# Four attention layers on one core: another order of the first block's maxima, and another opening of layer 0

## The chip, the cores and the metric

The kernel runs on one core of a Trainium2 chip. The metric is the device time of one execution in microseconds (us); the time of a version is the median of its runs. One execution was also profiled, and the profile's times count from the start of its span.

## What is computed

The input x holds 2048 tokens of 576 numbers (float32). Four layers follow each other, A, B, A, B, and each adds attention on the normalised x:

```python
x = x + A(layernorm(x)); x = x + B(layernorm(x))   # and once more
# A: q, k, v of 32 heads of 18 numbers each from wqkv
# B: 32 query heads, but one k and one v for all of them
p = softmax(einsum("bhqd,bhkd->bhqk", q, k) * 18 ** -0.5)
y = einsum("bhqk,bhkd->bhqd", p, v) @ wo
```

All 2048 x 2048 scores of every head are computed; nothing is masked.

## The kernel before

**Precision.** Operands are split into a high and a low part (fp32r), and a product takes the sum of high by high, high by low and low by high. A weight part is copied to its high part by one engine (`hi`) and its low part is subtracted by another (`lo`) in `load_w`, which `load_a` calls for layer A's weights, part by part and chunk by chunk of 128 rows (five chunks `c`; L229 is the subtraction).

**A layer's front.** x is normalised in 16 chunks of 128 tokens (`stats`, `scaled`: VectorE L309 to L321, with GpSimd L313 and L314 for the root), and each chunk is transposed by TensorE into PSUM (`transposed`: four products into a tile of the e banks, L272, and a fifth, L273, into `oacc` or, for chunks 1 and 3 of layer 0, into a tile of its own). `split_rows` brings it to SBUF as `xx` or `yx`: ScalarE copies the high part (L264, L265), VectorE subtracts for the low part (L266, L267). `advance` transposes the next chunk and prepares those behind it. `project(T, t)` forms 128 columns `t` of q and k for quarter `T` (512 tokens) by 14 products (`TERMS`, L439) in a PSUM tile psq; with `half` it does 256 tokens only. ScalarE then copies the result (ev, L447), VectorE or GpSimd makes its low part (L456, or L454 from the copy evr, L453), and SyncE stores it to DRAM (L499 to L503). In layer 0 `key_diff` adds a copy k0 (L473) on ScalarE for the key tiles. k and q come back from DRAM as rows of `big`, by columns, through `load_k` and `load_q` (L545).

**Maxima and exponentials.** For the softmax, each block `u` of 512 queries needs the maximum of its scores over all 2048 keys, per query. A product psm (`max_mm`, L613; `qc` counts 128 queries, `kb` 512 keys) gives 128 x 512 scores, and VectorE reduces them (L620). When 32 of them are there for a block, `max_final` takes the negated maximum (L752), GpSimd splits it (hl), `max_store` transposes it (L761) and stores it to DRAM (m_d, L763), and `max_rows` loads it as two further rows of `big` (L767), so that the product pse (L776) yields scores less the maximum. ScalarE takes the exponential (L785), and the product with the values gathers in `oacc` (L806). The main loop runs over 16 pairs of heads and four blocks, and its order is written out by hand in `UNIT`.

**Before the main loop.** The first `LEAD` = 14 groups of four psm have no exponentials beside them. `woven(max_pairs, left, every)` weaves them into the projections that are left: `beat` counts products of 512 columns, and after each `every` of them one group is issued. In A layers all 14 lie in the stretch `fill`; in B layers five lie in quarter 2, six in quarter 3 (`woven`, called with 5 and 10, then 1, 2 and 2 with 7, 6 and 6), and the rest in `fill`. Their order in B layers is the list `m_first` of (u, qc, kb): two entries for both heads of the pair make one group of four, called #1 to #14 here.

**PSUM.** Eight banks: three for `mtile`, four for `etile`, one for `oacc`. `etile` serves psq of the fill, the transposes and pse; `mtile` serves psm and the other psq. Each takes its banks in turn, and a new tile waits until the readers of the bank's last tile are done.

## Time and profile before

| | us |
|---|---|
| median of 3 runs | 5605.41 |
| the runs | 5609.56, 5603.79, 5605.41 |
| the profiled execution | 5606.94 |
| its span in the profile | 5605.2 |
| TensorE busy | 5579.4 |
| VectorE busy | 4943.0 |
| ScalarE busy | 4936.3 |
| GpSimd busy | 1741.9 |

The span leaves out 1.74 us around it. In a timeline row stand the start, the duration, the engine with line, operation, output and inputs, a count where rows are merged, and in brackets how long the engine stood idle before and what ended that. PE is TensorE, DVE VectorE, ACT ScalarE, POOL GpSimd, SPq SyncE's queue of DMA issues. A duration of merged rows runs to the modelled end of the last one, so that consecutive rows of PE overlap by a pipeline's depth.

### The profile page before, as it was taken

What the parts mean: (1) busy time and instruction counts of PE and PEld (TensorE: products, weight loads), DVE (VectorE), ACT (ScalarE), POOL (GpSimd) and SP (SyncE); (2) the same over time, 40 slices, a digit from 0 to 9 for tenths busy, and PEclk for the clock granted to TensorE, in tenths of its full rate; (3) what the DMA queues carried; (4) which work ended last, traced back from release to release, by engine and by line L of the source; (5) the groups of instructions that cost most, each with busy time, mean ns of one, the idle gap of its engine ahead of it and who ended that gap; (6) DMA issues with size and microseconds to landing.
All of it is one profiled execution on the core that took longest, in us unless ns stands there. A gap on an engine that the chain in (4) does not pass through costs nothing.

```text
span 5605.2 us, 138270 instructions
## 1 busy us (share of the span) xinstructions
PE 5579.4 (100%) x53372; PEld 2835.7 (51%) x53372; DVE 4943.0 (88%) x9513; ACT 4936.3 (88%) x9884; POOL 1741.9 (31%) x2236
## 2 busy tenths in 40 slices
PE   9999999999999999999999999999999999999999
PEld 7644444444844444444686444444448444444446
DVE  5799999998699999999747999999987999999995
ACT  3599999999389999999726999999992999999996
POOL 3142323234233232333421332323242333333332
PEclk9999999999999999999999999999999999999999
DMA  6311111111421000001253111111114201010102
GB/s 226 120 47 38 37 39 36 39 36 27 128 68 24 23 21 23 20 23 25 61 188 104 50 36 38 37 39 36 37 31 136 56 23 24 23 24 20 24 14 80
DMA packets 258556, 291.59 MB, mean 52 GB/s; under 512 B 132700, under 2 KB 172892, under 8 KB 248176
## 3 DMA queue, kind: packets, MB, share of 16 engines
q1 hardware_dynamic: 257896, 282.75, 18.0%
q8 instruction: 419, 6.86, 0.5%
q14 instruction: 241, 1.97, 0.1%
HBM read 158.77 MB, written 119.86 MB: 50 GB/s over the span
## 4 chain that ended last, share of the span: by engine, by line
PE 97%; ACT 1%; DVE 1%; DMA 0%; issue 0%; SPq 0%; POOL 0%; ACTq 0%; DVEq 0%; POOLq 0%
PE oacc L806 38%; PE pse L776 23%; PE psm L613 21%; PE psn L280 6%; PE psq L439 6%; PE psd L605 3%; ACT pt L785 1%; PE ps L272 0%; DVE mx L620 0%; DMA big<-m_d 0%; DMA m_d<-tr 0%; PE oacc L273 0%; SPq L763 0%; DVE mxd L620 0%; ACT side L785 0%
## 5 line engine op out<-in xcount | busy, mean ns | idle before, releaser
L620 DVE TENSOR_REDUCE mxd<-psm 128x1 f32<-128x512 f32 x5952 | 3750.1, 683 | 181.5 <-PE psd L605 64.9
L785 ACT ACTIVATE pt<-pse 128x512 f32<-128x512 f32 x6584 | 3578.4, 628 | 28.3 <-PE pse L776 1.5
L613 PE MATMUL psm<-big 62*128 62x512 f32 x7200 | 2504.4, 444 | 0.6
L776 PE MATMUL pse<-big 64*128 64x512 f32 x8192 | 2409.1, 431 | 7.2 <-DMA big<-m_d 3.1
L806 PE MATMUL oacc<-pt,vbuf 128*19 128x192 f32 (+6 forms) x20244 | 1794.5, 379 | 1.2 <-DVE oc L202 1.0
L776 PEld LDWEIGHTS pse<-big 64*128 64x128 f32 x8192 | 1209.2, 184 | 893.8 <-ACT pt L785 517.6
L613 PEld LDWEIGHTS psm<-big 62*128 62x128 f32 x7200 | 1132.7, 184 | 676.7 <-DVE mxd L620 262.2
L806 PE MATMUL oacc<-side,vbuf 128*19 128x64 f32 (+6 forms) x5004 | 1402.5, 377 | 0.0
L785 ACT ACTIVATE side<-pse 128x512 f32<-128x512 f32 x1608 | 998.4, 621 | 5.9
L202 POOL TENSOR_SCALAR hl<-neg 128x8 fp32r<-128x8 f32 x256 | 50.5, 197 | 2746.7 <-DVE neg L752 2746.7
L806 PEld LDWEIGHTS oacc<-pt,vbuf 128*19 128x19 f32 x20244 | 447.8, 97 | 604.8 <-issue 488.7
L617 DVE CUSTOM_DVE_ANT_0 side<-psm,side 128x512 f32<-128x512 f32 x992 | 681.1, 687 | 37.0 <-PE psm L613 8.6
L610 ACT ACTIVATE side<-psd 128x512 f32<-128x512 f32 x992 | 601.3, 648 | 1.3 <-PE psd L605 1.3
L806 PE MATMUL oacc<-pt,vy 128*19 128x384 f32 (+2 forms) x5700 | 587.2, 417 | 0.0
L829 POOL TENSOR_TENSOR rl<-lt,mone 128x8 f32<-128x8 f32 x256 | 422.9, 1652 | 350.2 <-DMA lt<-os 350.2
L806 PE MATMUL oacc<-side,vy 128*19 128x384 f32 (+2 forms) x1404 | 455.7, 415 | 0.0
L605 PE MATMUL psd<-kd,big 54*128 54x512 f32 x992 | 428.0, 472 | 0.0
L806 PEld LDWEIGHTS oacc<-side,vbuf 128*19 128x19 f32 x5004 | 317.4, 97 | 146.4 <-issue 119.8
L447 ACT ACTIVATE ev<-psq 128x512 fp32r<-128x512 f32 (+1 forms) x112 | 66.9, 598 | 319.1 <-PE psq L439 266.6
L842 POOL TENSOR_TENSOR os<-os,rb 96x512 f32<-96x512 f32 x256 | 328.2, 1282 | 19.8 <-DMA rb<-r_d 19.8
L820 POOL TENSOR_TENSOR os<-os,side 96x512 f32<-96x512 f32 x240 | 307.2, 1280 | 20.0
L202 POOL TENSOR_SCALAR os<-side 32x512 f32<-32x512 f32 x480 | 293.7, 612 | 40.1 <-POOL hl L756 0.4
(93 smaller groups left out, 3310.3 us busy)
## 6 DMA issues: line engine op xcount, KB each, us to landing
big<-qk_d SPq DMA_DIRECT2D x180, 432.0 KB
qk_d<-ev SPq DMA_DIRECT2D x96, 512.0 KB
qk_d<-ev SPq DMA_DIRECT2D x120, 256.0 KB
rb<-r_d SPq DMA_DIRECT2D x512, 36.0 KB
o_d<-os SPq DMA_DIRECT2D x512, 36.0 KB
m_d<-tr SPq DMA_DIRECT2D x1024, 2.0 KB
o<-o_d SPq DMA_DIRECT2D x64, 256.0 KB
big<-m_d SPq DMA_DIRECT2D x512, 4.0 KB
```

What stands on the lines that cost most here:

```text
L202: eng.tensor_scalar(dst, src, 1.0, 0.0, op0=OP.mult, op1=OP.add)
L280: nc.tensor.matmul(ps, lhs[:, xc, :], wsm[:, wc, h * 288:(h + 1) * 288], start=i == 0, stop=i == len(TERMS) - 1)
L439: nc.tensor.matmul(ps[:n].rearrange("p (u t) -> p u t", u=2)[:, us], w[:, wc, :n], xts[T][:, us, xc, :], start=(xc, wc) == TERMS[0], stop= ...
L605: nc.tensor.matmul(ps, q[b:b + 3 * DH, c0:c0 + P], kds[p if is_a else 0][b:b + 3 * DH], start=True, stop=True)
L610: nc.scalar.activation(r, ps, AF.Relu)
L613: nc.tensor.matmul(ps, q[b:b + KM, c0:c0 + P], k[b:b + KM, kb * 512:(kb + 1) * 512], start=True, stop=True)
L617: nc.vector.tensor_tensor_reduce(out=r, in0=ps, in1=r, scale=1.0, scalar=-3.0e38, op0=OP.add, op1=OP.max, accum_out=mx[:, r0:r0 + 1])
L620: nc.vector.reduce_max(mx[:, r0:r0 + 1], ps, axis=AX.X)
L776: nc.tensor.matmul(e, k[r:r + KE, kc * P:(kc + 1) * P], q[r:r + KE, u * 512:(u + 1) * 512], start=True, stop=True)
L785: nc.scalar.activation(pt, e, AF.Exp, scale=SCALE)
L806: nc.tensor.matmul(oacc[j:j + DH + 1, cs], v_of(kc)[:, 2 * p + a if is_a else 0, :], pts[p, u, i][:, cs], start=kc < 2 and c0 == 0, stop=k ...
L829: nc.gpsimd.tensor_tensor(rl, lts.pop((p, u)), mone, op=OP.pow)
```

## The change

1. `m_first` of the B layers lists block 0 whole before block 1's later keys, and `max_store` and `max_rows` of that block are called after 42 and 48 products rather than 46 and 50.
2. In each group of four psm before the main loop the first takes an `etile` (before: the fourth), the other three an `mtile`.
3. `FREE`, which sets how many beats the groups of `fill` are to be done ahead of its end, is 8 in A layers and stays 4 in B layers.
4. Layer 0 begins with half products of three tiles of columns, not two, with the transposes of chunks 2 and 3 between them; the whole product of tile 2 in quarter 0 goes.
5. GpSimd subtracts all five low parts of layer 0's first weight part; VectorE did two of them.
6. Layer 0's chunk 7 is transposed after tile 7 of quarter 0 rather than after tile 8.

```diff
-FREE = 4
+FREE = 8, 4
...
-        m_first = [] if is_a else ([(0, i // 2, i % 2) for i in range(8)] + [(1, i // 2, i % 2) for i in range(4)] +
-                                   [(0, i, 2) for i in range(4)] + [(1, i // 2, i % 2) for i in range(4, 6)] +
-                                   [(0, i, 3) for i in range(4)] + [(1, i // 2, i % 2) for i in range(6, 8)] +
-                                   [(1, i, 2) for i in range(4)] + [(1, i, 3) for i in range(4)])
+        def block(u, kb, qcs=range(4)):
+            return [(u, qc, kb) for qc in qcs]
+
+        m_first = [] if is_a else (block(0, 0) + block(0, 1) + block(1, 0) + block(0, 2) + block(0, 3) +
+                                   block(1, 1) + block(1, 2) + block(1, 3))
...
             for a in range(2):
-                max_mm(a, etile if m_done[0] % 4 == 3 else mtile)
-            if not is_a and m_done[0] == 46:
+                max_mm(a, mtile if m_done[0] % 4 else etile)
+            if not is_a and m_done[0] == 42:
                 max_store(0, 0)
-            elif not is_a and m_done[0] == 50:
+            elif not is_a and m_done[0] == 48:
                 max_rows(0, 0)
...
-                    load_a(c, (part,), nc.scalar, nc.gpsimd if part == 0 and c < 3 else nc.vector)
+                    load_a(c, (part,), nc.scalar, nc.vector if part else nc.gpsimd)
...
-            for terms in (TERMS_LO[:9], TERMS_LO[9:]):
-                for t in (0, 1):
-                    project(0, t, half=0, terms=terms)
-            more("trans", 4)
+            for t in range(3):
+                project(0, t, half=0, terms=TERMS_LO[:9])
+            for t in range(3):
+                project(0, t, half=0, terms=TERMS_LO[9:])
+                if t < 2:
+                    more("trans", 3 + t)
             ready(0)
             finish_loads(5)
-            for t in (0, 1):
+            for t in range(3):
                 project(0, t, half=1)
...
-                ts = range(0 if T or layer else 2, 9) if T < 3 else (6, 7, 8, 0, 4)
+                ts = (None, *range(3, 9)) if T + layer == 0 else range(9) if T < 3 else (6, 7, 8, 0, 4)
...
-                project(T, t, not is_a and T >= 2)
+                if t is not None:
+                    project(T, t, not is_a and T >= 2)
...
+                elif T + layer == 0:
+                    moves = i in (0, 2, 4, 5)
                 else:
-                    moves = i % 2 != (T + layer == 0) if is_a else i < 4
+                    moves = i % 2 if is_a else i < 4
...
-        woven(max_pairs, left, (work - FREE) / left)
+        woven(max_pairs, left, (work - FREE[layer % 2]) / left)
```

Three places show how the rows move. First TensorE in layer 0's opening, from the low terms to the second half products; psq is a projection's tile, ps_260 and ps_270 (before), ps_265 and ps_280 (changed) are the transposes of chunks 2 and 3. Before:

```order
L439 MATMUL psq<-yx,big 128x256 x13
L439 MATMUL psq<-yx,big 128x256 [waits Pool_49] x3
L439 MATMUL psq<-yx,big 128x256 [waits DVE_49] x2
L439 MATMUL psq<-yx,big 128x256 x5
L272 MATMUL ps_260<-ident,xh 128x128 [waits DVE_49]
...
L272 MATMUL ps_270<-ident,xh 128x128 [waits DVE_49]
...
L439 MATMUL psq<-yx,big 128x256 x19
L439 MATMUL psq<-yx,big 128x512 x14
```

With the change:

```order
L439 MATMUL psq<-yx,big 128x256 x22
L439 MATMUL psq<-yx,big 128x256 [waits Pool_49] x5
L272 MATMUL ps_265<-ident,xh 128x128 [waits DVE_49]
...
L439 MATMUL psq<-yx,big 128x256 x5
L272 MATMUL ps_280<-ident,xh 128x128 [waits DVE_49]
...
L439 MATMUL psq<-yx,big 128x256 x5
...
L439 MATMUL psq<-yx,big 128x256 x33
```

Nine more half products stand ahead of chunk 3's transposes, four of them ahead of chunk 2's, and the 14 products of 512 columns are gone.

Second, ScalarE at the end of quarter 0 in layer 0, where L264 and L265 split chunk 7 and the L447 and L473 beside them are the copies of tile 8. Before:

```order
L473 ACTIVATE k_614<-psq 128x512 [waits DMAHW6_49,DMAHW0_49,Pool_49]
L447 ACTIVATE ev<-psq 128x512 [waits DMAHW1_49,DMAHW7_49,PE_49,Pool_49]
L473 ACTIVATE k_637<-psq 128x512 [waits DMAHW6_49,Pool_49]
L264 ACTIVATE xx<-ps_642 128x4x128 [waits PE_49]
L265 ACTIVATE xx<-oacc 128x128 [waits PE_49]
```

With the change:

```order
L264 ACTIVATE xx<-ps_633 128x4x128 [waits PE_49]
L265 ACTIVATE xx<-oacc 128x128 [waits PE_49]
L447 ACTIVATE ev<-psq 128x512 [waits DMAHW1_49,DMAHW7_49,PE_49,Pool_49]
L473 ACTIVATE k_672<-psq 128x512 [waits DMAHW6_49,Pool_49]
L447 ACTIVATE ev<-psq 128x512 [waits DMAHW2_49,PE_49,Activation_49]
```

The split of chunk 7 moved past tile 8's two copies.

Third, TensorE in quarter 3 of layer 1, at groups #9 and #10; the DMA semaphores are those of the loads of k's columns 1536 to 2047, one for each head. Before:

```order
L613 MATMUL psm_23418<-big_81 128x512 [waits DVE_49]
L613 MATMUL psm_23421<-big_81 128x512 [waits DVE_49]
L613 MATMUL psm_23424<-big_81 128x512 [waits DVE_49]
L613 MATMUL psm_23427<-big_81 128x512 [waits PE_49,Activation_49]
L439 MATMUL psq_23411<-xx_23096,big_81 128x512 x6
L613 MATMUL psm_23436<-big_81 128x512 [waits DMAHW6_49,DVE_49]
L613 MATMUL psm_23439<-big_81 128x512 [waits DMAHW7_49,DVE_49]
L613 MATMUL psm_23442<-big_81 128x512 [waits DVE_49]
L613 MATMUL psm_23445<-big_81 128x512
```

With the change:

```order
L614 MATMUL psm_23432<-big_81 128x512 [waits DMAHW6_49,DVE_49]
L614 MATMUL psm_23435<-big_81 128x512 [waits DMAHW7_49,DVE_49]
L614 MATMUL psm_23438<-big_81 128x512 [waits DVE_49]
L614 MATMUL psm_23441<-big_81 128x512 [waits DVE_49]
L439 MATMUL psq_23425<-xx_23110,big_81 128x512 x6
L614 MATMUL psm_23450<-big_81 128x512 [waits PE_49,Activation_49]
L614 MATMUL psm_23453<-big_81 128x512 [waits DVE_49]
L614 MATMUL psm_23456<-big_81 128x512 [waits DVE_49]
L614 MATMUL psm_23459<-big_81 128x512 [waits DVE_49]
```

The first product that waits for these loads moved from group #10 to group #9, one group ahead.

## The prediction

> **What bounds the kernel now.** I read the page first (busy times, then the chain that ended last), then TensorE's waits, then the timeline around each wait that the change touches, then the stretches' granted clock.

> ```profile
> span 5605.2 us, 138270 instructions
> PE 5579.4 (100%) x53372; PEld 2835.7 (51%) x53372; DVE 4943.0 (88%) x9513; ACT 4936.3 (88%) x9884; POOL 1741.9 (31%) x2236
> PE 97%; ACT 1%; DVE 1%; DMA 0%; issue 0%; SPq 0%; POOL 0%; ACTq 0%; DVEq 0%; POOLq 0%
> ```

> TensorE is busy for 5579.4 of 5605.2 us: 25.8 us of idle time are all that any reordering can win, and the changed kernel's TensorE does the same work (14 products of 512 columns become 28 of 256). TensorE's waits by line:

> ```profile
> PE pse L776 <- DMA big<-m_d: 3.1, 4, 1.4
> PE psq L439 <- ACT xx L264: 1.9, 1, 1.9
> PE psq L439 <- DVE ev L456: 0.7, 1, 0.7
> ```

> The reader is to see how little there is: the change aims at the first (the maxima of a layer's first block must be back in DRAM before the first exponential's product) and at the second (chunk 7 in layer 0). I take its parts in program order.

> **Layer 0's opening.** TensorE:

> ```profile
> 12.03 5.38 PE L439 MATMUL psq<-yx,big 128*128 128x256 f32 x24 [0.22 <-DVE yx L267]
> 17.80 0.60 PE L272 MATMUL ps<-ident,xh 128*128 128x128 f32 x4
> 20.64 5.90 PE L439 MATMUL psq<-yx,big 128*128 128x256 f32 x34 [0.23 <-DVE yx L267]
> 26.37 0.60 PE L272 MATMUL ps<-ident,xh 128*128 128x128 f32 x4
> 26.81 0.27 PE L273 MATMUL oacc<-ident,xh 128*128 128x128 f32 x1
> 27.80 2.58 PE L439 MATMUL psq<-yx,big 128*128 128x512 f32 x10 [0.72 <-DVE ev L456]
> ```

> VectorE and GpSimd beside it:

> ```profile
> 7.31 3.00 POOL L229 TENSOR_TENSOR big<-raw,big 128x384 fp32r<-128x384 f32 x3
> 19.57 0.69 DVE L266 TENSOR_TENSOR yx<-ps,yx 128x512 fp32r<-128x512 f32 x1
> 20.61 0.82 DVE L309 BATCH_NORM_STATS2 st<-xo 128x6 f32<-128x288 f32 x2
> 27.06 1.89 DVE L456 TENSOR_TENSOR ev<-psq,ev 128x512 fp32r<-128x512 f32 x3
> ```

> GpSimd's two further low parts cost 1.00 us each and end at 7.31 + 5.00 = 12.3; their first reader comes after 27 half products, four of which ran before 12.03, so near 17.0: hidden by more than 4 us, and free. VectorE's two additions go, but VectorE waits for ScalarE's split of chunks 2 and 3 later on, so nothing comes of it.

> A product of 512 columns takes 0.2325 us (3.72 us for 16, in the next part's first two rows). From 20.64 to 26.37 stand 20 half and 14 full ones: (5.73 - 3.26) / 20 = 0.124 us a half one. Chunk 3's transposes now follow nine more half products, 9 x 0.124 = 1.1: they start at 18.9 instead of 17.80 and end at 19.5. ScalarE's copy (0.6) then ends at 20.1, and VectorE's split of chunk 3 starts at 20.13 instead of 19.57: **+0.56**. Behind it VectorE is busy without a gap to the low half of tile 0's result at 27.06, and in the same order after the change, so that ends at 28.3 and tile 3's first product, which needs its PSUM bank, starts at 28.35 instead of 27.80. TensorE meanwhile has less to do: 34 half products from 21.14 end at 25.4, the transposes at 26.1. So its idle time of 0.72 us becomes about **2.3**, and the work moved forward (14 x 0.124 = 1.7 us) is only waited out here. Bounds: nothing lost if ScalarE is quicker (0), or all of it and a slow clock (below).

> **Chunk 7.**

> ```profile
> 44.82 3.88 PE L439 MATMUL psq<-yx,big 128*128 128x512 f32 x16
> 48.54 0.60 PE L272 MATMUL ps<-ident,xh 128*128 128x128 f32 x4
> 46.64 0.29 DVE L267 TENSOR_TENSOR xx<-oacc,xx 64x128 fp32r<-64x128 f32 x1
> 48.79 0.60 ACT L447 ACTIVATE ev<-psq 128x512 fp32r<-128x512 f32 x1 [0.92 <-POOL wsm L229]
> 50.52 0.59 ACT L264 ACTIVATE xx<-ps 128x512 fp32r<-128x512 f32 x1
> 51.17 4.14 PE L439 MATMUL psq<-xx,big 128*128 128x512 f32 x10 [1.92 <-ACT xx L264]
> ```

> The wait of 1.92 us is ScalarE's order: chunk 7's split stands behind tile 8's two copies. The change puts it ahead of them, so this wait goes. What is late next: tile 8's 14 products (3.26 us) now come behind the transposes. Tile 7 ends at 48.54 - 3.26 + 0.55 = 45.8; four transposes to 46.3; the fifth writes oacc, which VectorE frees at 46.93 + 0.55 = 47.5 when it has read chunk 6 (a **new wait of 1.2 us**, with tile 8 queued behind it); tile 8 runs from 47.6 to 50.9, and the next quarter follows at once. 50.9 against 51.17: **-0.27** for the whole opening, -1.92 + 1.2 + 0.55, less 0.1 where pipelined ends overlap.

> **The clock.**

> ```profile
> 47.87:51.28 3.41, 1.49 (x10) 1.07 (x9) 1.63 (x5) 1.85 (x4) 3.18 (x5) 1.00 1.00 361
> 51.28:54.69 3.41, 3.41 (x9) 2.67 (x10) 3.33 (x7) 0.00 (x1) 2.97 (x7) 0.50 1.03 387
> 1563.38:1566.79 3.41, 3.41 (x14) 1.21 (x15) 1.13 (x4) 2.10 (x5) 0.40 (x2) 0.50 0.57 146
> 1566.79:1570.21 3.42, 3.42 (x28) 1.08 (x30) 2.28 (x4) 1.97 (x4) 0.00 (x0) 0.50 0.60 144
> ```

> The columns are the stretch, then PE, PEld, DVE, ACT and POOL, then PEclk. The clock is halved over 3.41 us behind a stretch with 1.49 us of TensorE work, and over 6.83 us in layer 1's start. The stretches begin 1512.10 us apart, 443 times 3.4134, so they lie on a grid that no edit here controls: 1.7 us lost per halved stretch of TensorE work, about 5 in this run. I leave those in the sum (the new idle times may put others in the place of the removed one) and keep 1.7 per new gap for the range. [...]

> **Layers 0 and 2: FREE and the tiles of the group.**

> ```profile
> 217.61 0.59 ACT L453 ACTIVATE evr<-psq 128x512 f32<-128x512 f32 x1
> 218.09 2.08 ACT L785 ACTIVATE pt<-pse 128x512 f32<-128x512 f32 x4
> 218.26 0.50 PE L776 MATMUL pse<-big 64*128 64x512 f32 x2 [0.59 <-ACT evr L453]
> ```

> The third pse waits 0.59 us for a PSUM bank that the last tile's copy frees; with the etile first in the group it comes one product later. But ScalarE goes from that copy straight into the exponentials (217.61 + 0.59, then 218.09) and TensorE's next work needs them, so ScalarE's chain sets the pace and the wait moves down it. Maxima moved up to four beats (4 x 0.2325 = 0.93 us) meet a VectorE with idle time. Between -0.59 and +0.25 each; I take -0.05 each, near none: **-0.1**.

> **Layers 1 and 3: the order of the maxima.** Groups of four products (psm, two blocks for two heads) are woven into the projections, #9 at 1543.60 and #10 at 1545.86.

> ```profile
> 1540.99 1.21 SPq L545 DMA_DIRECT2D big<-qk_d  x2
> 1543.60 0.73 PE L613 MATMUL psm<-big 62*128 62x512 f32 x4
> 1545.86 0.73 PE L613 MATMUL psm<-big 62*128 62x512 f32 x4
> 1543.60:1545.86 2.26, 2.26 (x12) 1.35 (x12) 1.75 (x4) 0.00 (x0) 0.72 (x1) 1.00 0.89 321
> 1553.05 6.63 DVE L620 TENSOR_REDUCE mx<-psm 128x1 f32<-128x512 f32 x11
> 1556.71 2.16 DMA big<-m_d
> 1558.91 0.73 PE L776 MATMUL pse<-big 64*128 64x512 f32 x4 [0.65 <-DMA big<-m_d]
> ```

> Block 0's maxima now end with group #10 instead of #11, and the stores follow 4 maxima sooner; at 0.6 us each (6.63 us for 11, without a gap) that covers 0.65, so the wait at 1558.91 goes. But the price is new: k's last quarter (columns 1536 to 2047) was first read by #10, and now **#9 reads it**. Its loads are issued at 1540.99 to 1542.20. #10 met no wait, so they land before 1545.86. The nearest landing, of 4 KB rows, took 2.16 us from its issue: not before 1542.20 + 2.16 = 1544.36. A wait at #9 of 0.76 to 2.26, then. The queues were busy to 0.89 in exactly this stretch, and these loads move 108 KB each: I take the upper part, **1.9**. Behind #9 in TensorE's order stand all later projections and groups, and VectorE, which is fed by them, slides as well. Net in layer 1: 1.9 - 0.65 = **+1.25**.

> ```profile
> 4334.42 1.22 SPq L545 DMA_DIRECT2D big<-qk_d  x2
> 4337.02 0.73 PE L613 MATMUL psm<-big 62*128 62x512 f32 x4
> 4339.28 0.73 PE L613 MATMUL psm<-big 62*128 62x512 f32 x4
> 4352.15 0.90 PE L776 MATMUL pse<-big 64*128 64x512 f32 x4 [0.47 <-DMA big<-m_d]
> ```

> Layer 3 repeats it: issue ends at 4335.64, so the wait at 4337.02 is 0.78 to 2.26; 1.9 - 0.47 = **+1.43**.

> **Sum.** The profiled execution took 5606.94 us (span 5605.2 and 1.74 around it): 5606.94 - 0.27 - 0.1 + 1.25 + 1.43 = 5609.25. It stands 1.53 above the median of the runs shown, so against that median **5607.7**.

> **Rivals.**
> - *It does what it is meant to.* The loads land by 0.76 after #9's turn or sooner, the waits for m_d and xx go. For it: 2.16 us sufficed for small rows. Against it: a busy queue. Two waits of 0.4 instead of 1.9 and one halved stretch less: 5607.7 - 3.0 - 1.7 = 5603.
> - *The clock takes more.* The gaps of 2.3 at 26 us and 1.9 at each #9 each may put one stretch at half speed: two of three give 5607.7 + 3.4 = 5611.1. For it: 51.28. Against it: the stretch must begin so that most of a gap lies in one.
> - *Clearly slower.* In layers 1 and 3 the ramp behind #9 is paced by VectorE; if #9's gap halves the clock and TensorE, in short pieces between waits, doesn't win it back until the first pse, 15 us later (1558.91), each layer loses four stretches of 1.7: 5607.7 + 13.6 = 5621. It decides from five halved stretches in all (8.5 us); the trace has two in a row at most.
> - *The edits do nothing at all*, since all of them sit behind other work: 5605.4. Against it: #9's operand is a plain dependence.

> **How the numbers follow.** A measurement of this kernel tells 0.2% (11.2 us) from no change, and hardly less. Chances: the forecast 0.46, as meant 0.18, the clock 0.24, nothing 0.07, clearly slower 0.04, faster by over 0.2% 0.01 (it would take nearly half of all idle time). The bounds of #9's wait (-2.3 to +0.7 in both layers together), of the layers 0 and 2 (-1.1 to +0.6) and a halved stretch more or less make 5602.5 to 5612.5; that leaves out the slowest rival and the clock's worst, under 2 in 10. So faster 0.02, same 0.93, slower 0.05.

> **What would show it.** Right: tile 3's first product near 28.35 behind 2.3 us idle, released by VectorE L456; the second quarter's first product near 50.9 with no wait for xx, and a wait of about 1.2 for VectorE at chunk 7's fifth transpose; a wait of TensorE's psm for the DMA big<-qk_d in layers 1 and 3, near 1.9 each; none for m_d at their first pse; the wait for evr smaller at 218 with the first oacc product no sooner. Wrong: no idle before #9, a stall longer than 2.3 there, or the m_d wait still in place behind it.

## The result, and the profile after

The changed kernel takes 5612.34 us (median of 22 runs, 5610.32 to 5618.38) against 5605.15 for the kernel before (22 runs, 5603.79 to 5610.19): a ratio of 1.0013, 95% interval 1.0007 to 1.0018. It is slower by 7.2 us, inside the 0.2% and inside the range, but 4.6 us above the forecast of 5607.7, and nearly at the range's end (5612.5). The interval leaves out 1, so these runs tell 0.13% from no change, where the prediction took 0.2% as the least that could be told.

The page of the changed kernel, its span and busy times, and then TensorE's waits by line (total, times, longest):

```profile
span 5610.5 us, 138287 instructions
PE 5584.6 (100%) x53386; PEld 2841.5 (51%) x53386; DVE 4944.5 (88%) x9511; ACT 4936.6 (88%) x9884; POOL 1745.4 (31%) x2238
```

```profile
PE pse L782 <- ACT pt L791: 3.6, 3, 2.1
PE psq L439 <- DVE ev L456: 2.3, 1, 2.3
PE pse L782 <- ACT evr L453: 2.2, 4, 0.6
PE psm L614 <- DMA big<-qk_d: 1.8, 4, 0.5
PE psq L439 <- DVE mx L621: 1.0, 2, 0.5
PE pse L782 <- DMA big<-m_d: 0.8, 2, 0.6
```

The two waits that the change aimed at are gone or small: xx is not in the list any more, m_d fell from 3.1 to 0.8. In their place stand the wait of 2.3 for VectorE in the opening, 1.8 for k's loads, 1.0 more for evr, 1.0 for VectorE's reductions (mx, before a projection in layers 1 and 3 each), and one of 2.1 that is put down to ScalarE's pt. And TensorE is busy for 5.2 us more, though it does the same work: a product that waits between its neighbours counts as busy here (group #8 below: 1.32 us of busy time for 0.73 before, and no wait listed), so the list of waits doesn't show all.

To find the rest I cut both traces at marks that both have: the first psq of a layer and its first product oacc<-pt,vbuf. Between them lies the layer's front, behind them its main loop. In us, the changed kernel less before: start -0.40; fronts of layers 0 to 3 -1.64, +2.38, +0.77, +2.62; loops +2.39, -3.11, +1.80, +0.50. The sum is +5.3, the difference of the spans; the profiled run of before stood 1.8 above its median and the changed one's (5612.24) at its own, which makes the 7.2.

The stretches of the changed kernel in which the clock was halved, and the one ahead of the last (the column behind POOL is PEclk):

```profile
27.96:31.38 3.42, 3.42 (x10) 2.65 (x9) 2.25 (x7) 0.00 (x0) 0.79 (x2) 0.50 1.03 380
219.11:222.52 3.41, 3.41 (x14) 1.21 (x16) 1.84 (x4) 2.63 (x6) 0.41 (x2) 0.50 0.53 151
222.52:225.94 3.42, 3.42 (x26) 1.37 (x24) 1.89 (x3) 1.57 (x3) 0.00 (x0) 0.50 0.60 158
4181.98:4185.40 3.42, 1.30 (x12) 0.48 (x4) 0.00 (x0) 2.91 (x7) 0.00 (x0) 1.00 0.06 9
4185.40:4188.81 3.41, 3.41 (x23) 1.02 (x20) 0.00 (x0) 1.84 (x4) 0.00 (x0) 0.50 0.06 22
```

Layer 0's loop has lost with 219.11 what layer 1's loop had lost with 1563.38 in the trace of before: those two terms (+2.39, -3.11) are where a halved stretch happened to fall. Two fronts of before hold such time too: layer 1's the first 0.9 us of that stretch (it ends at 1564.30), and layer 0's the one at 51.28. The four other kernels below with the old opening, which have none there, take 210.1 to 210.9 us for layer 0's front, where before took 212.0; so most of the -1.64 is that stretch's. What remains and is new: the fronts of layers 1 to 3, and layer 2's loop.

**Fronts.** TensorE of the changed kernel in layer 1, groups #8 and #9 and the start of the main loop:

```profile
1541.32 1.32 PE L614 MATMUL psm<-big 62*128 62x512 f32 x4
1545.74 0.47 PE L614 MATMUL psm<-big 62*128 62x512 f32 x1 [0.52 <-DMA big<-qk_d]
1546.69 0.70 PE L614 MATMUL psm<-big 62*128 62x512 f32 x3 [0.47 <-DMA big<-qk_d]
1562.68 0.49 PE L782 MATMUL pse<-big 64*128 64x512 f32 x1 [0.51 <-ACT evr L453]
```

Group #9 waits for k as predicted, 1.0 us rather than 1.9 (0.8 in layer 3), and evr now ends last at the first pse, 0.5, where m_d did. The surprise is the first row: group #8's four products, which took 0.73 us before, take 1.32, and no wait is listed. The weight loads (PEld), which stand ahead of their products, show it:

```profile
1540.81 2.48 DVE L621 TENSOR_REDUCE mx<-psm 128x1 f32<-128x512 f32 x4
1541.32 0.41 PEld L614 LDWEIGHTS psm<-big 62*128 62x128 f32 x3 [0.36 <-issue]
1542.14 0.18 PEld L614 LDWEIGHTS psm<-big 62*128 62x128 f32 x1 [0.41 <-DVE mx L621]
```

The group's fourth product stands until VectorE has reduced one more tile: the last of group #7's four reductions ends at 1542.08, the product starts at 1542.14. VectorE works as before (2.48 us for four reductions in both traces); what changed is which banks the group's four tiles lie in.

### The profile page after: what moved, and what is told of

It is laid out like the page before. It is cut to its first block, busy times and chain, and to the rows that moved or that the text cites. A ratio compares the mean times of both kernels' runs of the same rounds, so it can differ in the third digit from the quotient of the medians.

```text
span 5610.5 us, 138287 instructions
## 1 busy us (share of the span) xinstructions
PE 5584.6 (100%) x53386; PEld 2841.5 (51%) x53386; DVE 4944.5 (88%) x9511; ACT 4936.6 (88%) x9884; POOL 1745.4 (31%) x2238
## 3 DMA queue, kind: packets, MB, share of 16 engines
q14 instruction: 241, 1.97, 0.1%
## 4 chain that ended last, share of the span: by engine, by line
PE 96%; DVE 1%; ACT 1%; DMA 0%; issue 0%; SPq 0%; POOL 0%; ACTq 0%; POOLq 0%; DVEq 0%
PE oacc L812 38%; PE pse L782 22%; PE psm L614 21%; PE psn L280 6%; PE psq L439 5%; PE psd L606 3%; DVE mx L621 1%; ACT pt L791 0%; PE ps L272 0%; DMA big<-qk_d 0%; DMA m_d<-tr 0%; DVE ev L456 0%; PE oacc L273 0%; DVE mxd L621 0%; ACT side L791 0%
## 5 line engine op out<-in xcount | busy, mean ns | idle before, releaser
L447 ACT ACTIVATE ev<-psq 128x512 fp32r<-128x512 f32 (+1 forms) x112 | 66.9, 597 | 325.2 <-PE psq L439 277.7
## 6 DMA issues: line engine op xcount, KB each, us to landing
qk_d<-ev SPq DMA_DIRECT2D x120, 256.0 KB
o<-o_d SPq DMA_DIRECT2D x64, 256.0 KB
```

## Experiments

Four theories. **Depth**: with the etile first, the group's other three tiles are the three mtiles, and the last of them can be written only when the fourth reduction of the group before is done; with the etile last, the third reduction is enough. TensorE may run ahead of VectorE by one tile less, 0.6 us. **Loads**: the loss is k's quarter at #9. **Clock**: halved stretches behind new gaps. **Code**, formed after the first four runs, is told at its place. Each version was timed in 5 rounds beside the kernel before; medians of before were 5605.35 (beside the first four versions that were run), 5605.15 (beside the next four: b_opening_new, b_count, a_count, a_k_early) and 5606.10 (beside the last four).

| version | median us | ratio, 95% interval | front of layer 1 | 2 | 3 | wait at the end of layer 2's loop |
|---|---|---|---|---|---|---|
| before (profile) | 5605.15 | | 94.98 | 200.93 | 94.52 | 0.7 |
| change | 5612.34 | 1.0007 to 1.0018 | 97.36 | 201.70 | 97.14 | 2.1 |
| a_tile_old | 5609.49 | 1.0000 to 1.0017 | 97.52 | 201.22 | 97.13 | 2.3 |
| a_order_old | 5613.95 | 1.0005 to 1.0023 | 96.56 | 201.80 | 97.43 | 2.3 |
| b_tile_new | 5609.79 | 1.0000 to 1.0017 | 96.49 | 201.47 | 96.34 | 0.7 |
| b_order_new | 5608.72 | 0.9998 to 1.0015 | 97.08 | 200.95 | 95.90 | 0.8 |
| b_opening_new | 5604.93 | 0.9992 to 1.0010 | 94.66 | 201.24 | 94.70 | 1.8 |
| b_count | 5607.25 | 0.9995 to 1.0013 | 95.03 | 201.23 | 94.60 | 1.9 |
| a_count | 5611.40 | 1.0002 to 1.0019 | 97.51 | 201.67 | 97.04 | 1.3 |
| a_k_early | 5610.68 | 0.9999 to 1.0017 | 96.49 | 201.98 | 96.71 | 2.0 |
| opening_count | 5605.50 | 0.9992 to 1.0009 | 94.59 | 201.23 | 94.81 | 0.6 |
| best1 | 5603.60 | 0.9988 to 1.0005 | 94.31 | 200.93 | 94.07 | 1.9 |
| best1_count | 5602.60 | 0.9987 to 1.0004 | 94.35 | 200.93 | 94.13 | 0.6 |
| b_free_new | 5606.76 | 0.9994 to 1.0012 | 95.09 | 201.22 | 94.76 | 0.7 |

A halved stretch can add to a front in which it falls (a_tile_old has one each in layers 1 and 3, b_order_new one in layer 1). Where it falls on the end of layer 2's front it adds 0.3: a_tile_old, b_opening_new, b_count, opening_count and b_free_new have one there, and 201.22 to 201.24, where the kernels with the old tile order and none there have 200.93 to 200.95. It falls otherwise from kernel to kernel. The intervals are 6 to 10 us wide, so that differences of 1 to 3 us between two medians are not shown by the times alone; the places in the traces carry more.

**The tile order, undone and alone.** a_tile_old is the changed kernel with

```diff
-                max_mm(a, mtile if m_done[0] % 4 else etile)
+                max_mm(a, etile if m_done[0] % 4 == 3 else mtile)
```

and b_tile_new the kernel before with the reverse.

> The changed kernel with one thing undone: the fourth psm of a group takes the etile again, not the first. Theory 1 (depth): with the etile first, the last mtile of a group can start only when all four reductions of the group before are done, not three, so TensorE stands 0.1 to 0.5 us in many groups: 0.8 us in each of layers 0 and 2, 1.2 in each of layers 1 and 3, 4.0 in all. It expects 5612.3 - 4.0 = 5608.3, and groups of four psm in layer 2's fill at the old pitch without a wait for reductions. Theory 2 (loads): the loss is k's last quarter at group #9 and what slides behind it; the tile order is free: 5612. Theory 3 (clock): halved stretches behind the new gap at 26 us and elsewhere: 5612.

> The kernel before with the etile first in each group and nothing else. Theory 1: +4.0 against before, 5609. Theory 2 and theory 3: no change, 5605.

By the medians it brings 2.9 us undone and costs 4.4 alone. Alone, with the order of the maxima as before and nothing waiting for k, layer 1's groups read:

```profile
1542.69 1.30 PE L613 MATMUL psm<-big 62*128 62x512 f32 x4
1546.52 0.73 PE L613 MATMUL psm<-big 62*128 62x512 f32 x4
1548.79 1.30 PE L613 MATMUL psm<-big 62*128 62x512 f32 x4
1554.31 1.33 PE L613 MATMUL psm<-big 62*128 62x512 f32 x4
1557.15 1.19 PE L613 MATMUL psm<-big 62*128 62x512 f32 x4
```

These are groups #8, #9, #10, #12 and #13. #8, #10 and #12, which took 0.73, 0.73 and 0.78 before, start 2.24 to 2.27 us behind the group ahead of them, sooner than VectorE has done its four reductions (2.48 us), and take 1.30 to 1.33. #9 and #11 follow by 3.83 and 3.28 us and keep 0.73; #13 goes from 1.11 to 1.19. The fronts of layers 1 and 3 are 1.5 and 1.8 us longer than before's, and against b_opening_new, whose front of layer 1 (94.66) has no halved stretch in it, the first is 1.8 too. Layer 2's is 0.5 longer. In layer 2's fill of the changed kernel two groups that follow each other take 0.76 and 0.81:

```profile
2990.27 0.76 PE L614 MATMUL psm<-big 62*128 62x512 f32 x4
2993.02 0.81 PE L614 MATMUL psm<-big 62*128 62x512 f32 x4
```

and in a_tile_old, at the same place:

```profile
2989.94 0.73 PE L614 MATMUL psm<-big 62*128 62x512 f32 x4
2992.66 0.73 PE L614 MATMUL psm<-big 62*128 62x512 f32 x4
```

Layer 2's 14 groups, each from its first product's start to its last one's end, take 10.22 us in all in before, 10.82 in b_tile_new and 11.04 in the changed kernel. That is +0.60 and +0.82, beside +0.54 and +0.77 in the front. This is what the depth theory said, though it had 0.8 in each of layers 0 and 2 and 1.2 in each of layers 1 and 3; the other two have no reading for it.

**The order of the maxima, undone and alone.** a_order_old takes the old `m_first` and the stores after 46 and 50; b_order_new puts the new ones into the kernel before.

```diff
-        m_first = [...block 1's (1, 1) and (1, 2) between block 0's...]
+        m_first = block(0, 0) + block(0, 1) + block(1, 0) + block(0, 2) + block(0, 3) + block(1, 1) + ...
-            if not is_a and m_done[0] == 46:
+            if not is_a and m_done[0] == 42:
```

> The changed kernel with the old order of the maxima in layers 1 and 3 (and the stores after 46 and 50 products). Theory 1: the order costs 1.0 + 0.8 us at group #9 and gives back 0.65 + 0.47 at the first pse, so undoing it brings 0.7: 5611.6. Theory 2: it is the whole loss: 5605.5. Theory 3: 5612.

> The kernel before with the new order of the maxima (and stores after 42 and 48 products) and nothing else. Theory 1: +0.7, 5605.9, with the wait for the DMA big<-qk_d at group #9 and none for m_d at the first pse. Theory 2: +6, 5611. Theory 3: 5605.

Alone it costs 3.4 us by the medians, where the depth theory had 0.7 (the interval, 0.9998 to 1.0015, covers both). Among TensorE's waits in it are, in layer 1 and then in layer 3:

```profile
PE psm L614 <- DMA big<-qk_d: 1.3, 2, 0.8
PE pse L777 <- ACT evr L453: 0.5, 1, 0.5
```

```profile
PE psm L614 <- DMA big<-qk_d: 1.5, 2, 1.1
PE pse L777 <- ACT evr L453: 0.5, 1, 0.5
```

These are 1.3 and 1.5 where the prediction took 1.9, and a wait for evr of 0.5 in m_d's place, which it did not have. In layer 3, whose front has no halved stretch, it grew by 95.90 - 94.52 = 1.38 (the prediction said 1.43, with two errors that cancel). Together with the tile order #9 comes later and waits less, 1.0 and 0.8. Undoing it in the changed kernel should have brought 0.7; it was 1.6 slower by the medians, with the clock halved in five places of its profile and an interval that covers the changed kernel's. Its front of layer 1, with no halved stretch in it, is 0.8 shorter than the changed kernel's, where the theory has 0.35 (1.0 - 0.65); layer 3's has one in it and is 0.3 longer. Why the time rose stays open.

**k's load ahead of the queries' stores** (a_k_early, the changed kernel with)

```diff
                 store(ev_f, 96, 96 + DH, D, t0)
+                if T == 3:
+                    load_k(0, T * 512, T * 512 + 512)
                 store(ev_f, 0, 64, 512, t0)
```

(and no load of it behind the second store).

> The changed kernel with the load of k's last quarter issued right behind the stores of that quarter, ahead of the two stores of the queries' columns, in layers 1 and 3. Where the wait at group #9 is the loads' landing, issuing them about 1.0 us sooner takes it away (1.0 and 0.8 us): 5612.3 - 1.8 = 5610.5. Where other traffic holds them, it stays and the time too.

The median is 1.7 us lower, which is inside the noise, but the DMA big<-qk_d is gone from TensorE's waits in layers 1 and 3, and the fronts are 0.9 and 0.4 shorter. The loads were late by their place in SyncE's queue.

**The opening alone** (b_opening_new: parts 4 to 6 of the change, the rest as before), and what it does 4170 us later. The three profiles so far of kernels with the new opening (the change, a_tile_old, a_order_old) had a long wait at the end of layer 2's loop; b_tile_new and b_order_new had not. There the last block's four stores of m_d must land before the load that the last pse needs. The changed kernel, SyncE's queue, TensorE, and the DMA queues from 4178 to 4184:

```profile
4178.73 1.91 SPq L769 DMA_DIRECT2D m_d<-tr  x4
4183.21 0.52 SPq L773 DMA_DIRECT2D big<-m_d  x2
4184.66 1.28 PE L782 MATMUL pse<-big 64*128 64x512 f32 x4 [2.12 <-ACT pt L791]
```

```profile
q1 hardware_dynamic: 342, 0.09, 8.1%
q8 instruction: 1, 0.02, 1.3%
```

and the kernel before (from 4178.5 to 4184.5):

```profile
4179.01 1.91 SPq L763 DMA_DIRECT2D m_d<-tr  x4
4182.03 0.52 SPq L767 DMA_DIRECT2D big<-m_d  x2
4183.48 0.99 PE L776 MATMUL pse<-big 64*128 64x512 f32 x4 [0.67 <-ACT pt L785]
```

```profile
q1 hardware_dynamic: 480, 0.10, 9.6%
```

The load is issued 4.5 us behind the first store instead of 3.0. In the changed kernel one packet of the queue "instruction" moved in that stretch, in the kernel before none. The page of before counts 419 such packets of 16 KB; TensorE's 106,744 products and weight loads make 255 a packet, and from one packet to the next it issues 256.0 instructions on the average, those that only wait for a semaphore among them, so I read the packets as its code, fetched in order. The opening adds 14 products, with weight loads 28 instructions, and each later piece comes that much earlier in the program: 4180.5 instead of 4184.7, on top of the stores. It lasts to 4181.75, and the landings of the stores show what it does. Each store lands in 16 parts. Before, the 16 parts of each store land within 0.17 us, the last at 4181.91. In the changed kernel 15 parts of each do so, but one part of the second, third and fourth store lands 2.1, 1.8 and 1.5 us behind its fellows, the last at 4183.09, and the load is issued at 4183.21. The releaser pt is the profile's guess: the product waits for ScalarE and for the load, and it starts 0.13 us behind the load's landing both before (4183.35) and with the change (4184.53).

> The kernel before with the new opening of layer 0 and chunk 7's new place (parts 4 to 6 of the change), and the rest as before. Theory 4 (code): TensorE's instructions come in pieces of 16 KB by DMA; the opening's 14 more products (28 instructions with their weight loads) make every later piece come some 3 to 4 us earlier, and at the end of layer 2's main loop one then meets the four m_d stores, whose landing delays the last block's rows by about 1.5 us: TensorE waits 2.1 to 2.3 us there instead of 0.7, and the clock halves behind it. It expects layer 2's main loop 1.8 us longer than before, and 5605.3 - 1 + 1.8 to 3.2 = 5607. The prediction's step: 5605.1, and no such wait.

> The kernel before with 14 throwaway transposes of 18 x 128 into oacc, first in TensorE's order, where it waits 6.4 us for the first chunk anyway; nothing else. Theory 4: they shift the code's pieces as the opening does, so the wait of 2.1 to 2.3 us at the end of layer 2's main loop appears, though layer 0 is unchanged: 5605.3 + 2 = 5607. Otherwise: 5605.3 and a wait of 0.7.

b_count is the kernel before with instructions alone:

```diff
+            for _ in range(14):
+                nc.tensor.transpose(oacc[:, :DH], ident[64:82, :], ident[64:82, 64:82])
             more("trans", 2)
```

Their result is overwritten, and they run while TensorE waits for the first chunk anyway. Its DMA queues from 4175.5 to 4181.5, and its last pse:

```profile
q8 instruction: 1, 0.02, 1.1%
```

```profile
4176.19 1.91 SPq L765 DMA_DIRECT2D m_d<-tr  x4
4180.48 0.52 SPq L769 DMA_DIRECT2D big<-m_d  x2
4181.93 1.08 PE L778 MATMUL pse<-big 64*128 64x512 f32 x4 [1.92 <-DMA big<-m_d]
```

With no change of layer 0's order the wait went from 0.67 to 1.92, and the profile now names m_d. The time, 5607.25 as forecast, would not show it alone, since its interval (0.9995 to 1.0013) covers no change. The opening alone has the wait too (1.8), but no halved stretch behind it, and at 5604.93 instead of 5607 it is as fast as before. So the opening gains about what the code's new place loses.

> The changed kernel with the same 14 throwaway transposes. Theory 4: the piece that met the m_d stores at 4180.5 comes some 4 us earlier still, ahead of the stores, and the wait at the end of layer 2's main loop is back at 0.7: 5612.3 - 2 = 5610. Otherwise: 5612.3, with the wait of 2.1.

> The kernel before with the new opening and chunk 7's new place, and 20 throwaway transposes first in TensorE's order. Theory 4 (code): 40 instructions carry the piece that met the m_d stores at 4175 some 5 us ahead of them, so the wait at the end of layer 2's main loop falls from 1.8 to 0.7, and layer 0 stays as in the run with the opening alone: 5604.9 - 1.1 = 5603.8. Otherwise: 5604.9.

With 28 more products than before (a_count) the piece came at 4178.7, still beside the stores' issue (2.48 us instead of 1.91), and the wait was 1.3, not 0.7; the time fell by 0.9, not 2. With 34 (opening_count, 20 throwaway transposes) it came ahead of the stores (4171.5) and the wait was 0.6, but the median was 5605.50 instead of 5603.8. The clock was halved in four places of that profile, and the runs of before beside it had risen by 0.95, so the missing gain is inside the noise. Over all 14 profiles the waits sort by the count alone: 1.8 to 2.3 in the seven kernels with 14 products more, 0.6 to 0.8 in those with none or 34, 1.3 with 28.

**FREE alone** (b_free_new: `FREE = 8, 4` in the kernel before).

> The kernel before with FREE = 8 in layers 0 and 2 alone. The prediction's step: between -0.6 and +0.25 in each, near none: 5605.2. Theory 1 adds that denser groups (7.93 beats instead of 8.21) meet VectorE's reductions only when the tile order holds one bank back, so alone they cost nothing: fronts of layers 0 and 2 unchanged within 0.2 us.

Layer 2's front is 0.3 longer, as in b_count, which has the old FREE and a halved stretch at the same place; the median is 0.7 above before's, in the noise. Alone it costs nothing that shows. With the tile order beside it, layer 2's front is 201.70 (201.67 in a_count) instead of 201.47, so 0.2 may be its part there.

**What is left when the costs are dropped.** best1 takes the new opening, the new order with k's load ahead, and the tile order and FREE of before; best1_count adds 20 throwaway transposes.

> The parts that held nothing against them, together: the new opening and chunk 7, the new order of the maxima with the load of k's last quarter issued ahead of the queries' stores, but the tile order and FREE of before. Theories 1 and 2: no wait at group #9 and none of 0.65 and 0.47 for m_d at the first pse of layers 1 and 3: 5604.9 - 1.1 = 5603.8, layers 1 and 3's fronts 94.1 and 94.1 us. If the other waits of VectorE take its place, 5605.

> The same with 20 throwaway transposes first in TensorE's order. Theory 4: a wait of 0.7 for m_d at the end of layer 2's main loop instead of about 1.8, 1.1 us less than without them: 5602.7.

5603.60 and 5602.60 beside 5606.10 for before are the two fastest versions. Their intervals (0.9988 to 1.0005, 0.9987 to 1.0004) don't exclude no change against before; against the changed kernel they are about 9 us faster. They lie within 0.2 us of the forecasts, in part by luck: those counted from runs beside a before of 5605.15, so that they meant gains of 1.35 and 2.45, and the gains are 2.5 and 3.5. best1_count at the start of layer 1's main loop, and its wait at the end of layer 2's:

```profile
1557.22 0.61 PE L786 MATMUL pse<-big 64*128 64x512 f32 x2 [0.52 <-ACT evr L453]
4177.84 1.15 PE L786 MATMUL pse<-big 64*128 64x512 f32 x4 [0.63 <-ACT pt L795]
```

The wait at the front's end is now for evr, ScalarE's copy of the last projection, not for a DMA.

## Why the prediction came out as it did

- **The whole.** A change within 0.2% was forecast with 0.93, and so it came, but as +7.2 instead of +2.3. Two terms that the sum lacked, the tile order in the groups and the code, make most of the difference. That the time still lies in the range is partly luck: the terms named for it (-2.3 to +0.7, -1.1 to +0.6 and one halved stretch of 1.7) reach from 5602.6 to 5610.7, and nothing there adds up to its upper end of 5612.5. The premise was too narrow as well: it counted idle time alone, and TensorE's busy time rose by 5.2 us at the same work.
- **The opening.** The gap came as worked out, 2.27 us and released by VectorE's L456, but at 26.91 instead of 28.35. TensorE's timeline of the changed kernel:

```profile
11.64 4.79 PE L439 MATMUL psq<-yx,big 128*128 128x256 f32 x28 [0.23 <-DVE yx L267]
23.93 0.60 PE L272 MATMUL ps<-ident,xh 128*128 128x128 f32 x4
26.91 3.33 PE L439 MATMUL psq<-yx,big 128*128 128x512 f32 x9 [2.27 <-DVE ev L456]
46.37 0.27 PE L273 MATMUL oacc<-ident,xh 128*128 128x128 f32 x1
49.73 13.18 PE L439 MATMUL psq<-xx,big 128*128 128x512 f32 x56
```

The wait for xx went, and the second quarter follows at once. From the first psq to there it is 49.73 - 10.19 = 39.5 us against 51.17 - 10.59 = 40.6: -1.0, where -0.27 was predicted. The start went faster (28 half products took 4.79 us, 24 took 5.38 before): they follow each other by 0.21 us up to the profile's first record of the granted clock and by 0.12 behind it, and that record stands at 14.31 here and at 17.15 before. The stretch at 27.96 behind the gap was halved, but the 1.7 that the range had kept for it was not lost. The new wait of 1.2 for oacc is missing here, since TensorE was late by that stretch; a_tile_old, without it, shows 1.13 in its timeline:

```profile
46.73 0.33 PE L273 MATMUL oacc<-ident,xh 128*128 128x128 f32 x1 [1.13 <-DVE xx L267]
```

All nine kernels with the new opening have the gap (2.27 to 2.32 us), and five of them a halved stretch behind it. From the first psq to the second quarter those five take 39.3 to 39.9 us, the other four 39.8 to 40.3. That the sum counts no halved stretch behind the gap was a guess, which no run had shown. In the changed kernel the clock fell to 0.50 at 27.96 behind 2.27 us of waiting, and at 4185.40 behind a stretch with 1.30 us of work.
- **FREE and the tiles: the step that failed.** "With the etile first in the group it comes one product later [...] Between -0.59 and +0.25 each; I take -0.05 each": I looked at the one wait at the main loop's start and not at the 14 groups before it. At that one place nothing was gained: the wait for evr moved to the fourth pse and is 0.57 instead of 0.59. Layer 2's front grew by 0.77, of which 0.5 are the tile order, and in layers 1 and 3, where I had not priced the edit at all, it costs 1.5 to 1.8 alone. That is the largest single term of the loss.
- **The order of the maxima.** Mechanism and place were right: #9 waits for k's last quarter, in both layers, and the m_d wait goes. The size of 1.9 was too large (1.3 and 1.5 alone, 1.0 and 0.8 in the change), and a successor of 0.5, evr, was not named.
- **Not in the prediction: the code.** The changed kernel's TensorE "does the same work", I wrote; but the 14 products more are 28 instructions more, and instructions have a place in time too. It cost 1.1 to 1.6 us of waiting at the end of layer 2's loop where the two met as in the change, and in the changed kernel a halved stretch lies behind it: +1.80 for that loop.
- **The rivals.** "The clock takes more" lies nearest in time (5611.1), and the stretch at 27.96 was as it said; but that one cost nothing, and the fronts show that most of the loss was not the clock's. "As meant" and "nothing" fell; "clearly slower" didn't happen, with never more than two halved stretches in a row.

## What to carry to other kernels

When a buffer's pool is changed for one product of a group, count how many products the producer can be ahead of the consumer before and after, for every group and not for the one place that the edit aims at: one tile less cost 4 us here. It shows in how long a group takes (0.73 to 1.30 us), and hardly in a list of waits: those of layer 1's psm weight loads for reductions are 2.6 us with the change and 3.0 before. Price a reordering by the latest operand that each moved instruction reads, and look at what is queued ahead of its load; moving that load cost nothing. And when few DMA waits are left, an edit that adds instructions moves every later piece of code (28 of them brought the piece at 4184.7 to 4180.5 here): compare where the packets of the instruction queue fall beside the small stores that something waits for.

## What the runs showed of the hardware

Halved stretches lay in 13 of the 14 profiles before the end of the program: behind a gap in layer 0's front or at the end of layer 2's loop, behind group #9's wait, and near the starts of the main loops, where the gaps in before and in the changed kernel are no longer than 0.7 us. Whether a gap of about 2 us has one behind it goes with where the grid of 3.41 us cuts it. The 14 profiles have 21 gaps of 1.8 to 2.4 us behind the first record of the clock. In eight of them at least 2.04 us lie in one stretch of the grid (the changed kernel's 24.64 to 26.91 lies whole in 24.55 to 27.96), and all eight have a halved stretch behind them. In eight others the grid leaves at most 1.68 us in any one stretch (a_tile_old's 25.20 to 27.52 is cut at 26.19), and none has. Of the five between, with 1.88 to 1.92 us in one stretch, three have. This is sorted from the profiles; no run moved a gap on the grid on purpose.
